# The causal mask of the 384-column score group, moved from four small matmuls to the bias table

## The chip, the core and the metric

One core of one Trainium2 chip runs the whole kernel. The metric is the device time of one execution in microseconds. Three executions of the kernel before took 774.68, 775.28 and 776.92 us; the median is 775.28 us.

## What is computed

Eight batches of eight heads of causal attention (576 positions, head size 64) with a bias that falls with a running sum, then a mixture of eight experts where each token goes to one expert.

```
scores = scale * q @ k.T                       # per head, 576 x 576
cum    = cumsum(max(s, 0))
bias   = -(cum[i] - cum[j])
scores = where(j > i, -1e9, scores + min(bias, 0))
attn   = softmax(scores)                       # rows
o      = attn @ v                              # then heads side by side: 4608 x 512
out[t] = gate[t] * relu(o[t] @ w1[e]) @ w2[e]  # e = argmax of o[t] @ w_gate
```

## The kernel before

Two heads make a pair; there are 32 pairs, worked on one after the other for the first 300 us. After them come the eight experts, which the change doesn't touch. Queries are cut into five groups, named by their number g: rows 128 g to 128 g + 127 for g = 0 to 3, and the last 64 rows of both heads together for g = 4. Group g needs the keys up to its own rows only, so its score widths are 128, 256, 384, 512 and 576 (`TW`, L57).

For each pair and group these steps follow each other:

- S (`scores`, L253, matmuls at L238): TensorE writes the scores of both heads to a PSUM tile named `s`. Each product is made of three terms, high by high, high by low and low by high halves of q and k (`kh`, `kl`). The pool of `s` tiles has two buffers, and the routing of tokens takes buffers of it too (below).
- R (`rowmax`, L278, instruction at L296): VectorE adds the bias table `B` to the scores, scales, and finds the row maximum. There is one instruction per head for g = 0 to 3 (R20 and R21 for group 2) and one for g = 4 (R40), each with a short read of its accumulator behind it.
- X (`expo`, L301): ScalarE takes the exponential. T (`trans`): TensorE turns the result. E (L334 on VectorE, L335 on ScalarE): the turned result is copied to `aT`. AV (`av`, L337): TensorE multiplies with v; XB (`keep`): VectorE copies that product out of PSUM (`xb`).

`B` has one tile per pair with four buffers. For each head it holds six blocks of 128 columns (`UB` = 768): blocks 0 to 3 hold the running sums of the keys, and GpSimd (`causal`, L176) writes masked copies of blocks 0 and 1 to blocks 4 and 5 and masks block 3 in place. Group 0 reads block 4, group 1 blocks 0 and 5, group 3 blocks 0 to 3. Group 2 would need blocks 0 and 1 and a masked block 2, which isn't there: block 2 is needed unmasked by group 3. So TensorE adds the mask of group 2: in `mms` (L227), ahead of the third term, four bf16 matmuls per pair (L233) add the product of `eye` and `tri`, a constant triangle, to the last 128 columns of the scores.

The order of all steps on all engines is written out by hand (`ORDER`, L33): one line of names with a pair offset each, gone through once per pair. On TensorE one pass reads

```
S0:0 [routing] T2:1 T4:1 S2:0 S4:0 T3:0 [routing] T1:0 S3:-1 T0:0 S1:-1 AV:1
```

where `:-1` is the next pair and `:1` the one before. From pair 6 on, each pass holds two routing steps, and each takes an `s` buffer, so the seven users of the two buffers alternate: S2 waits until R00 and R01 have read the buffer of S0, S4 until the first routing step's tile is read, and S3 until R40 has read the buffer of S4. On VectorE the same pass reads XB, R00, R01, a routing copy, E4 (the copy of 640 columns at L334), R20, R21, R40, a routing copy, then R31, R10, R30, R11 of the next pair and E0. The routing steps repeat every four pairs.

`table` (L164) loads `B` from memory by three transfers on SyncE's queue, four pairs ahead; `split` (L200) makes the q and k halves on GpSimd, two pairs ahead. GpSimd's pass is: the select and add of `causal`, `q` (L207), its low half (L212), `qd` (L222), `kl` (L219), and one or two scatters of routed tokens.

Of the kernel before, what the change touches and what calls it, by code (L numbers as in the profile page):

```python
# [8 lines left out]
F32 = mybir.dt.float32  # L9
F32R = mybir.dt.float32r  # L10
BF16 = mybir.dt.bfloat16
# [3 lines left out]
ALU = mybir.AluOpType  # L15
# [4 lines left out]
P, HP = 128, 64  # L20
B, H, S, D = 8, 8, 576, 64
# [33 lines left out]
TURN_AT = {0: 0, 2: 2}  # L55
PIN = True
TW = (128, 256, 384, 512, 576)  # L57
UB, UW = 768, 1536


def disjoint(tc, key, inst):
# [15 lines left out]
class Attention:  # L77
# [18 lines left out]
    def open_pairs(self):  # L96
        nc, rt, ident, low = self.nc, self.rt, self.K["ident"], self.Es[0][:, 0]
        cp, s, raw, cum, zz = self.first
        x = self.ldx.tile([P, 2 * S], F32, name="qk")
        self.st[0] = dict(x=x)  # L100
        for h, e in enumerate((nc.sync, nc.scalar)):
            e.dma_start(x[:, S * h : S * h + S], self.qkv[0][:, S * h : S * h + S])
        for h, e in enumerate((nc.sync, nc.scalar)):
            e.dma_start(raw[64 * h : 64 * h + 64], s)
        self.load(1)
        self.load_v(0)
        self.load(2)
        nc.vector.memset(zz, 0.0)
        nc.scalar.activation(self.sm.tile([P, 1], F32, name="m"), zz[:, :1], AF.Exp)
        nc.gpsimd.memset(low, 0.0)  # L110
        for h in range(2):
            self.keep_causal(low[64 * h : 64 * h + 64], low[64 * h : 64 * h + 64], [[-1, P]])
        self.mixed = cp.tile([P, HP], F32, name="mixed")
        nc.gpsimd.tensor_copy(self.mixed, low[:, :HP])
        b = self.st[0]["B"] = self.tab.tile([P, UW + S], F32, name="B")
        nc.gpsimd.memset(b, 0.0)
        self.causal(0)
        warm = self.ps_s.tile([P, 2, 512], F32, name="s")[:, 0]
        zb = zz.bitcast(BF16)
        for _ in range(WARM):  # L120
            nc.tensor.matmul(warm, zb[:, :P], zb[:, P : P + 512], start=True, stop=True)
        self.cum = cum
        self.sel = cp.tile([P, 3, P], F32, name="sel")
        for x, h, c in (0, 0, slice(0, P)), (1, 65, slice(0, P)), (2, 0, slice(0, HP)), (2, 1, slice(HP, P)):
            nc.vector.tensor_copy(self.sel[:, x, c], ident[:, h : h + 1].broadcast_to([P, c.stop - c.start]))
        self.eye = cp.tile([P, 3, HP], BF16, name="eye")
        nc.vector.memset(self.eye, 0.0)
        nc.vector.tensor_tensor(out=self.eye[:, 1], in0=ident[:, :HP], in1=ident[:, HP:], op=ALU.add)
        self.tri = cp.tile([P, P], BF16, name="tri")
        nc.vector.tensor_copy(self.tri, low)  # L130
        nc.vector.tensor_scalar(out=raw, in0=raw, scalar1=0.0, scalar2=8.0, op0=ALU.max, op1=ALU.mult)
        nc.vector.tensor_tensor_scan(
            out=cum, data0=raw, data1=zz, initial=0.0, op0=ALU.add, op1=ALU.add
        )
        for part in (0, 2, 1, 3, 4):
            self.split(0, part)
        nc.scalar.dma_start(self.K["cum"], cum[:64])
        self.table(1)
        self.load(3)
        self.table(2)  # L140
        self.load_v(1)
        self.table(3)
        self.load_v(2)
        for g in ORD[:2]:
            self.first_bias(g)
        nc.gpsimd.memset(self.Es[MIX][:, S:], 0.0)
        self.LT = rt.tile([P, 640], F32, name="LT", bufs=1)
        nc.gpsimd.memset(self.LT[:, S:], 0.0)
        self.xb, self.sums, self.sumx, self.rr, self.ra = [], [], [], [], []
        for i in range(2):  # L150
            self.xb.append(rt.tile([P, 4, 640], F32, name=f"xb{i}", bufs=1))
            nc.gpsimd.memset(self.xb[i][:, :, S:], 0.0)
            self.sums.append(rt.tile([P, 4, 8], F32, name=f"sums{i}", bufs=1))
            self.sumx.append(rt.tile([P, 4], F32, name=f"sumx{i}", bufs=1))
            self.rr.append(rt.tile([P, 5, 8], F32, name=f"rr{i}", bufs=1))
            nc.gpsimd.memset(self.rr[i][:, 4], 1.0)
            self.ra.append(rt.tile([P, 2, 5, 4], F32, name=f"ra{i}", bufs=1))
# [6 lines left out]
    def table(self, p):  # L164
        nc, cum = self.nc, self.K["cum"]
        t = self.st.setdefault(p, {})["B"] = self.tab.tile([P, UW + S], F32, name="B")
        nc.sync.dma_start(
            t[:, :UW].rearrange("p (h c) -> p h c", h=2)[:, :, :512],
            cum[2 * p : 2 * p + 2, :512].unsqueeze(0).broadcast_to([P, 2, 512]),
        )  # L170
        for h in range(2):
            nc.sync.dma_start(
                t[64 * h : 64 * h + 64, UW:], cum[2 * p + h : 2 * p + h + 1].broadcast_to([64, S])
            )

    def causal(self, p):  # L176
        t = self.st[p]["B"]
        b = t[:, :UW].rearrange("p (h k c) -> p h k c", h=2, c=P)
        self.keep_causal(b[:, :, 4:], b[:, :, :2], [[0, 2], [0, 2], [-1, P]])
        self.keep_causal(b[:, :, 3], b[:, :, 3], [[0, 2], [-1, P]])  # L180
        x = t[:, UW + 512 :]
        self.nc.gpsimd.tensor_tensor(out=x, in0=x, in1=self.mixed, op=ALU.add)

# [40 lines left out]
                    compare_op=ALU.is_ge, fill=0.0, base=base, channel_multiplier=2 * h - 1,  # L224
                )

    def mms(self, groups, diagonal=None, begin=True):  # L227
        for n in range(len(groups[0][1])):
            if n == diagonal:
                for out, eye, tri in ((P, 1, P), (HP, 0, HP)):  # L230
                    for h, (ps, _) in enumerate(groups):
                        r = slice(64 * h, 64 * h + 64)
                        self.nc.tensor.matmul(  # L233
                            ps[:, ps.shape[1] - out :], self.eye[r, eye : eye + 2], self.tri[r, :tri],
                            start=False, stop=False, skip_group_check=True,
                        )
            for out, terms in groups:
                self.nc.tensor.matmul(  # L238
                    out, terms[n][0], terms[n][1], start=begin and n == 0, stop=n == len(terms) - 1, skip_group_check=True
                )  # L240
# [12 lines left out]
    def scores(self, p, g):  # L253
        d = self.st[p]
        w = TW[g]
        if p == 0:
            if ("S", g) not in d:
                self.first_bias(g)
            ps = d["S", g]
        else:  # L260
            ps = d["S", g] = self.ps_s.tile([P, 2, 512], F32, name="s")
        if g == MIX:
            qh, ql = (self.qd[p % 2][:, x].rearrange("p h c -> p (h c)") for x in range(2))
            for a in range(2):
                c = slice(288 * a, 288 * a + 288)
                self.mms([(ps[:, a, :288], [
                    (qh, d["kh"][:, c]), (qh, d["kl"][:, c]), (ql, d["kh"][:, c]),
                ])], begin=p > 0)
            return
        groups = []  # L270
        for h in range(2):
            r = slice(64 * h, 64 * h + 64)
            qh, ql = (d["q"][r, x, P * g : P * g + P] for x in range(2))
            kh, kl = d["kh"][r, :w], d["kl"][r, :w]
            groups.append((ps[:, h, :w], [(qh, kh), (qh, kl), (ql, kh)]))
        self.mms(groups, 2 if g == 2 else None, p > 0)

    def rowmax(self, p, g, h):  # L278
        nc, d, w = self.nc, self.st[p], TW[g]
        ps, t = d["S", g], d["B"]  # L280
        if g == MIX:
            cut = lambda x: x.rearrange("p (a c) -> p a c", a=2)
            units = [(ps[:, :, :288], cut(t[:, UW:]))]
        else:
            cut = lambda x: x
            b = t[:, UB * h : UB * h + UB]
            if g == 1:
                cut = lambda x: x.rearrange("p (k c) -> p k c", c=P)
                b = cut(b)[:, 0:6:5]
            else:  # L290
                b = b[:, 512:640] if g == 0 else b[:, :w]
            units = [(cut(ps[:, h, :w]), b)]
        for x, mask in units:
            z = self.wk.tile([P, S], F32, name="z")
            m = self.sm.tile([P, 1], F32, name="m")
            nc.vector.tensor_tensor_reduce(  # L296
                out=cut(z[:, :w]), in0=x, in1=mask, scale=-0.125, scalar=3.0e38, op0=ALU.add, op1=ALU.min, accum_out=m,
            )
            d["z", g, h] = z, m
# [723 lines left out]
```

## Time and profile before

| what | value |
|---|---|
| median of three executions | 775.28 us |
| the profiled execution, its own time | 778.14 us |
| its span, first to last instruction | 776.4 us |
| mean granted TensorE clock | 0.992 |
| PE busy | 746.7 us (96%) |
| DVE busy | 453.9 us (58%) |
| ACT busy | 418.8 us (54%) |
| POOL busy | 251.7 us (32%) |

PE, DVE, ACT and POOL are TensorE's matmuls, VectorE, ScalarE and GpSimd; SPq is the queue of SyncE, which issues transfers. Busy shares are means over the whole span, attention and experts together. A row of the timeline has the start and the length in us, the engine, the line, the operation, what it writes and reads, its shape, and how many instructions were merged; in brackets stands the idle time of the engine before it and what ended it. Matmuls overlap, and their ends are modelled, so start-to-start distances are the safer measure on PE.

### The profile page before, as it was taken

What the parts mean: (1) busy time and instruction counts of PE and PEld (TensorE: products, weight loads), DVE (VectorE), ACT (ScalarE), POOL (GpSimd) and SP (SyncE); (2) the same over time, 40 slices, a digit from 0 to 9 for tenths busy, and PEclk for the clock granted to TensorE, in tenths of its full rate; (3) what the DMA queues carried; (4) which work ended last, traced back from release to release, by engine and by line L of the source; (5) the groups of instructions that cost most, each with busy time, mean ns of one, the idle gap of its engine ahead of it and who ended that gap; (6) DMA issues with size and microseconds to landing.
All of it is one profiled execution on the core that took longest, in us unless ns stands there. A gap on an engine that the chain in (4) does not pass through costs nothing.

```text
span 776.4 us, 17542 instructions
## 1 busy us (share of the span) xinstructions
PE 746.7 (96%) x6654; PEld 579.6 (75%) x6654; DVE 453.9 (58%) x1232; ACT 418.8 (54%) x1004; POOL 251.7 (32%) x362
## 2 busy tenths in 40 slices
PE   7899999999999997998999999999999999999995
PEld 4667777777777765687887888888888887878874
DVE  6778989888898985752363634422632453634420
ACT  4999999999999986441341523322512432513400
POOL 5665777676767664111001010010011001010011
PEclk9999999999999999999999999999999999999998
DMA  7999677776867543498161634510720442620101
GB/s 245 341 322 294 207 249 225 236 228 211 253 209 237 168 169 125 132 296 285 49 228 71 211 128 161 179 41 18 244 96 28 140 178 69 219 97 22 54 30 41
DMA packets 58015, 130.78 MB, mean 168 GB/s; under 512 B 5487, under 2 KB 6511, under 8 KB 57904
## 3 DMA queue, kind: packets, MB, share of 16 engines
q1 hardware_dynamic: 49216, 105.08, 42.2%
q0 software_dynamic: 5936, 18.92, 6.5%
q10 hardware_dynamic: 2752, 5.33, 2.1%
q8 instruction: 66, 1.08, 0.6%
q14 instruction: 45, 0.37, 0.2%
HBM read 101.30 MB, written 28.27 MB: 167 GB/s over the span
## 4 chain that ended last, share of the span: by engine, by line
issue 40%; PE 38%; DMA 11%; another core or an unknown queue 4%; POOL 3%; POOLq 1%; ACT 1%; DVE 1%; SPq 1%; ACTq 0%; DVEq 0%
PE s L238 12%; PE t L345 10%; PE t L312 7%; DMA out_dram<-y,xr 6%; PE ph L730 3%; PE py L752 3%; POOL out_dram L759 3%; PE s L312 1%; DMA qk<-in_qkv_dram 1%; PE s L388 1%; DMA B<-cum 1%; DMA xr<-xs 1%; DMA aT<-in_s_dram 1%; DMA raw<-in_w_dram 1%
## 5 line engine op out<-in xcount | busy, mean ns | idle before, releaser
L752 PE MATMUL py<-w2t,hT 128*128 128x512 f32 x768 | 181.3, 393 | 1.6 <-PEq L866 1.6
L730 PE MATMUL ph<-xT,w1t 128*128 128x512 f32 x768 | 178.3, 392 | 1.6 <-ACT xT L635 1.2
L308 ACT ACTIVATE E<-z,m 128x512 f32<-128x512 f32 (+4 forms) x288 | 166.8, 583 | 19.7 <-DVE m L296 16.9
L730 PEld LDWEIGHTS ph<-xT,w1t 128*128 128x128 f32 x768 | 143.8, 188 | 33.6 <-issue 2.5
L759 POOL DMA_INDIRECT out_dram<-y,xr x39 | 38.0, 975 | 398.3 <-DVE y L758 333.2
L752 PEld LDWEIGHTS py<-w2t,hT 128*128 128x128 f32 x768 | 142.5, 188 | 31.8 <-issue 2.0
L296 DVE CUSTOM_DVE_ANT_0 z<-s,B 128x512 f32<-128x512 f32 (+3 forms) x224 | 116.5, 543 | 13.2 <-PE s L238 4.7
L345 PE MATMUL t<-aT,v 128*64 128x64 f32 (+4 forms) x1152 | 94.6, 318 | 1.1 <-ACT w1t L657 1.0
L238 PE MATMUL s<-kh,q 64*128 64x128 f32 (+3 forms) x512 | 92.3, 370 | 2.7 <-DVE m L296 2.7
L758 DVE TENSOR_SCALAR y<-py,xr 128x512 f32<-128x512 f32 x35 | 26.3, 751 | 115.1 <-PE py L752 115.1
L732 ACT ACTIVATE hT<-ph 128x512 fp32r<-128x512 f32 x64 | 38.2, 597 | 102.3 <-PE ph L730 102.2
L733 DVE SCALAR_TENSOR_TENSOR hT<-ph,hT 128x512 fp32r<-128x512 f32 x64 | 44.1, 691 | 66.7 <-ACT hT L732 66.7
L312 PE MATMUL t<-ident,E 64*128 64x64 f32 x1600 | 75.4, 227 | 1.9 <-ACT aT L335 0.9
L335 ACT COPY aT<-t 128x1024 f32<-128x1024 f32 (+2 forms) x97 | 73.7, 795 | 6.4 <-PE t L312 6.3
L312 PEld LDWEIGHTS t<-ident,E 64*128 64x128 f32 x1600 | 63.8, 139 | 16.7 <-issue 5.3
L238 PEld LDWEIGHTS s<-kh,q 64*128 64x128 f32 x512 | 52.0, 186 | 29.8 <-DVE aT L334 23.5
L345 PEld LDWEIGHTS t<-aT,v 128*64 128x64 f32 x1152 | 50.5, 137 | 21.4 <-issue 11.1
L308 ACT ACTIVATION_READ_ACCUMULATOR E<-z,m 128x1 f32 x288 | 55.4, 192 | 0.0
L474 POOL DMA_INDIRECT xs<-xr,dsi x40 | 40.0, 999 | 37.1 <-DVE num L974 16.4
L635 ACT ACTIVATE xT<-t 128x512 fp32r<-128x512 f32 x32 | 17.5, 597 | 63.6 <-PE t L702 63.3
L219 POOL TENSOR_TENSOR kl<-qk,kh 128x576 fp32r<-128x576 f32 x30 | 42.6, 1420 | 25.0 <-ACT kh L215 25.0
L334 DVE COPY aT<-t 128x256 f32<-128x256 f32 (+1 forms) x63 | 38.7, 614 | 10.5 <-PE t L312 10.5
(159 smaller groups left out, 965.5 us busy)
## 6 DMA issues: line engine op xcount, KB each, us to landing
raw<-in_w_dram SPq DMA_DIRECT2D x32, 1024.0 KB, 5.6
qk<-in_qkv_dram SPq DMA_DIRECT2D x31, 576.0 KB, 5.3
B<-cum SPq DMA_DIRECT2D x31, 512.0 KB, 4.9
v<-in_qkv_dram SPq DMA_DIRECT2D x32, 320.0 KB, 3.9
B<-cum SPq DMA_DIRECT2D x62, 144.0 KB, 5.1
xr<-xs SPq DMA_DIRECT2D x7, 1028.0 KB, 5.5
xs<-blank ACTq DMA_DIRECT2D x9, 514.0 KB, 8.9
xs<-blank SPq DMA_DIRECT2D x8, 514.0 KB, 8.3
```

The source lines that it names most:

```text
L219: e.tensor_tensor(out=d["kl"], in0=k, in1=d["kh"].bitcast(F32), op=ALU.subtract)
L238: self.nc.tensor.matmul(out, terms[n][0], terms[n][1], start=begin and n == 0, stop=n == len(terms) - 1, skip_group_check=True)
L296: nc.vector.tensor_tensor_reduce(out=cut(z[:, :w]), in0=x, in1=mask, scale=-0.125, scalar=3.0e38, op0=ALU.add, op1=ALU.min, accum_out=m,)
L308: nc.scalar.activation(out, z[:, :w], AF.Exp, bias=m, scale=-1.0, accum_out=total)
L312: self.nc.tensor.transpose(out, src[r], self.K["ident"][r, r])
L335: return self.nc.scalar.copy(o, i)
L345: nc.tensor.matmul(ps[64 * h : 64 * h + 64, bank, lo - 512 * bank : hi - 512 * bank], v[:, kt, h], self.aT[p % 2][:, kt, h, lo:hi], start= ...
L474: ins = self.nc.gpsimd.indirect_dma_start(out=self.K["xs"], out_offset=IndirectOffsetOnAxis(ap=r["dsi"][:n, k : k + 1], axis=0), in_=r["xr ...
L730: nc.tensor.matmul(ps, w[:, a, d, c], x[:, b, d], start=n == 0, stop=n == 11)
L733: nc.vector.scalar_tensor_tensor(out=h[:, 1, f], in0=ps, scalar=0.0, in1=h[:, 0, f].bitcast(F32), op0=ALU.max, op1=ALU.subtract)
L752: self.nc.tensor.matmul(ps, hT[:, a, f, c], w[:, b, f % 4], start=f == 0 and i == 0, stop=f == 7 and i == 2)
L759: disjoint(self.tc, "out", self.nc.gpsimd.indirect_dma_start(out=self.out, out_offset=IndirectOffsetOnAxis(ap=row[:, DM + 1 : DM + 2].bitc ...
```

## The change

The table of each head gets a seventh block (`UB` = 896). The running sums of key blocks 0 and 1 lie in places 0 and 1, those of blocks 2 and 3 in places 3 and 4. GpSimd writes masked block 2 to place 2, masks place 4 in place, and writes masked blocks 0 and 1 to places 5 and 6. Group 2 then reads places 0 to 2 in one piece, and group 3 reads places 0, 1, 3 and 4 as two pieces. The four mask matmuls and their constants are gone. The transfer of both heads' first 512 sums becomes two transfers, one per head, each in pieces of 256 sums. The constant `sel`, used for the first pair alone, moves into a part of `aT` that isn't in use yet.

```diff
-UB, UW = 768, 1536
+UB, UW = 896, 1792
...
-        self.sel = cp.tile([P, 3, P], F32, name="sel")
+        self.sel = self.aT[1].rearrange("p a h c -> p (a h c)")[:, 3 * S : 3 * S + 3 * P].rearrange("p (x c) -> p x c", x=3)
...
-        self.eye = cp.tile([P, 3, HP], BF16, name="eye")
-        nc.vector.memset(self.eye, 0.0)
-        nc.vector.tensor_tensor(out=self.eye[:, 1], in0=ident[:, :HP], in1=ident[:, HP:], op=ALU.add)
-        self.tri = cp.tile([P, P], BF16, name="tri")
-        nc.vector.tensor_copy(self.tri, low)
...
-        nc.sync.dma_start(
-            t[:, :UW].rearrange("p (h c) -> p h c", h=2)[:, :, :512],
-            cum[2 * p : 2 * p + 2, :512].unsqueeze(0).broadcast_to([P, 2, 512]),
-        )
+        for h in range(2):
+            nc.sync.dma_start(
+                t[:, UB * h : UB * h + 768].rearrange("p (a c) -> p a c", a=2)[:, :, :256],
+                cum[2 * p + h, :512].rearrange("(a c) -> a c", a=2).unsqueeze(0).broadcast_to([P, 2, 256]),
+            )
...
-        self.keep_causal(b[:, :, 4:], b[:, :, :2], [[0, 2], [0, 2], [-1, P]])
-        self.keep_causal(b[:, :, 3], b[:, :, 3], [[0, 2], [-1, P]])
+        self.keep_causal(b[:, :, 5:], b[:, :, :2], [[0, 2], [0, 2], [-1, P]])
+        for x, y in (2, 3), (4, 4):
+            self.keep_causal(b[:, :, x], b[:, :, y], [[0, 2], [-1, P]])
...
-            if n == diagonal:
-                for out, eye, tri in ((P, 1, P), (HP, 0, HP)):
-                    for h, (ps, _) in enumerate(groups):
-                        r = slice(64 * h, 64 * h + 64)
-                        self.nc.tensor.matmul(
-                            ps[:, ps.shape[1] - out :], self.eye[r, eye : eye + 2], self.tri[r, :tri],
-                            start=False, stop=False, skip_group_check=True,
-                        )
...
-                b = cut(b)[:, 0:6:5]
+                b = cut(b)[:, 0:7:6]
+            elif g == 3:
+                cut = lambda x: x.rearrange("p (a c) -> p a c", a=2)
+                b = b[:, :768].rearrange("p (a c) -> p a c", a=2)[:, :, :256]
             else:
-                b = b[:, 512:640] if g == 0 else b[:, :w]
+                b = b[:, 640:768] if g == 0 else b[:, :w]
```

On PE, at groups 2 and 4 of one pair in the routing stretch, the order before has the weights and products of the mask between the second and the third term of the 384-column scores (`eye` and `tri` are the constants of the mask):

```order
L312 MATMUL t<-ident,E_109 128x64 x10
L238 MATMUL s<-kh,q 128x384 x2
L238 MATMUL s<-kl,q 128x384 x2
L233 LDWEIGHTS eye
L233 MATMUL s<-tri,eye 128x128
L233 LDWEIGHTS eye
L233 MATMUL s<-tri,eye 128x128
L233 LDWEIGHTS eye
L233 MATMUL s<-tri,eye 128x64
L233 LDWEIGHTS eye
L233 MATMUL s<-tri,eye 128x64
L238 MATMUL s<-kh,q 128x384 x2
```

On PE at the same place, the order of the change:

```order
L304 MATMUL t<-ident,E_109 128x64 x10
L227 MATMUL s<-kh,q 128x384 x2
L227 MATMUL s<-kl,q 128x384 x2
L227 MATMUL s<-kh,q 128x384 x2
L227 MATMUL s<-kh,qd_104 128x288
```

The third term now follows the second directly; nothing else of TensorE's order has moved.

On GpSimd, at the table of pair 1 early in the program, the order before (`mixed` is the mask of group 4, `ramp` a constant of the routing):

```order
L160 AFFINE_SELECT B<-B 128x2x256
L160 AFFINE_SELECT B<-B 128x2x128
L182 TENSOR_TENSOR B<-B,mixed 128x64
L207 CAST q<-qk 128x576
L212 TENSOR_TENSOR q<-qk,q 128x576
L905 IOTA blank 128x1
L912 IOTA ramp 128x8
```

On GpSimd at the same place, the order of the change:

```order
L155 AFFINE_SELECT B<-B 128x2x256
L155 AFFINE_SELECT B<-B 128x2x128 x2
L179 TENSOR_TENSOR B<-B,mixed 128x64
L204 CAST q<-qk 128x576
L209 TENSOR_TENSOR q<-qk,q 128x576
L897 IOTA blank 128x1
L904 IOTA ramp 128x8
```

There is one more select of 2 x 128 columns ahead of everything else that GpSimd does in the pass.

On SyncE's queue, at the first table, the order before and then that of the change (`qk` is the q and k of a pair to come):

```order
L167 DMA B<-cum 128x2x512
L172 DMA B<-cum 64x576 x2
L186 DMA qk<-in_qkv_dram 128x1152
L167 DMA B<-cum 128x2x512
L172 DMA B<-cum 64x576 x2
```

```order
L163 DMA B<-cum 128x2x256 x2
L168 DMA B<-cum 64x576 x2
L183 DMA qk<-in_qkv_dram 128x1152
L163 DMA B<-cum 128x2x256 x2
L168 DMA B<-cum 64x576 x2
```

Each table is issued in four transfers instead of three, and all behind it on that queue stand one issue later.

## Rows read from the trace of the kernel before

**Rows 1.** Busy time by stretch: us, then PE, PEld, DVE, ACT, POOL, clock, DMA

```profile
62.00:302.00 240.00, 237.81 (x3659) 175.11 (x3657) 209.07 (x748) 217.64 (x591) 165.12 (x239) 1.00 0.68 217
```

**Rows 2.** Timeline, PE and DVE, pair 16: S2, mask, S4, R20 to S3

```profile
157.81 0.34 PE L238 MATMUL s<-kl,q 64*128 64x384 f32 x2
...
157.98 0.26 PE L233 MATMUL s<-tri,eye 64*128 64x128 bf16 x4
157.99 0.81 DVE L334 COPY aT<-t 128x640 f32<-128x640 f32 x1
...
158.08 0.42 PE L238 MATMUL s<-kh,q 64*128 64x384 f32 x2
...
158.72 0.55 DVE L296 CUSTOM_DVE_ANT_0 z<-s,B 128x384 f32<-128x384 f32 x1
...
159.19 0.29 PE L238 MATMUL s<-kh,qd 128*128 128x288 f32 x1
159.19 0.08 DVE L296 DVE_READ_ACCUMULATOR2_ANT m<- 128x1 f32 x1
159.19 0.55 DVE L296 CUSTOM_DVE_ANT_0 z<-s,B 128x384 f32<-128x384 f32 x1
...
159.67 0.08 DVE L296 DVE_READ_ACCUMULATOR2_ANT m<- 128x1 f32 x1
159.72 0.76 DVE L296 CUSTOM_DVE_ANT_0 z<-s,B 128x576 f32<-128x576 f32 x1
...
160.40 0.08 DVE L296 DVE_READ_ACCUMULATOR2_ANT m<- 128x1 f32 x1
...
160.63 0.50 PE L238 MATMUL s<-kh,q 64*128 64x512 f32 x2
```

**Rows 3.** Waits on VectorE between 60 and 272 us: sum, times, longest

```profile
DVE xb L334 <- PE t L345: 10.1, 23, 0.7
```

**Rows 4.** Timeline, PE and DVE, pair 18: E4, R20, S4, R40, S3

```profile
176.25 0.82 DVE L334 COPY aT<-t 128x640 f32<-128x640 f32 x1 [1.24 <-PE t L312]
...
177.12 0.56 DVE L296 CUSTOM_DVE_ANT_0 z<-s,B 128x384 f32<-128x384 f32 x1
...
177.66 0.29 PE L238 MATMUL s<-kh,qd 128*128 128x288 f32 x1
...
178.08 0.08 DVE L296 DVE_READ_ACCUMULATOR2_ANT m<- 128x1 f32 x1
178.19 0.76 DVE L296 CUSTOM_DVE_ANT_0 z<-s,B 128x576 f32<-128x576 f32 x1
...
179.10 0.50 PE L238 MATMUL s<-kh,q 64*128 64x512 f32 x2
```

**Rows 5.** Groups by line and shape, to 400 us: busy, mean ns, idle before

```profile
L296 DVE CUSTOM_DVE_ANT_0 z<-s,B 128x512 f32<-128x512 f32 x64 | 44.0, 688 | 7.9 <-ACT aT L335 4.4 <-PE s L238 1.3 <-POOL qd L222 0.9
...
L296 DVE CUSTOM_DVE_ANT_0 z<-s,B 128x384 f32<-128x384 f32 x64 | 33.0, 551 | 4.0 <-PE s L238 3.4 <-ACT E L308 0.2
...
L296 DVE CUSTOM_DVE_ANT_1 z<-s,B 128x256 f32<-128x256 f32 x64 | 26.9, 420 | 3.2 <-ACT E L308 1.5 <-PE s L238 0.6
...
L160 POOL TENSOR_SCALAR_AFFINE_SELECT B<-B 128x256 f32<-128x256 f32 x32 | 13.0, 405 | 0.0
```

**Rows 6.** Timeline, GpSimd, pair 17: the tightest wait ahead of `q`

```profile
167.36 0.66 POOL L207 CAST q<-qk 128x576 fp32r<-128x576 f32 x1 [0.37 <-PE s L238]
```

**Rows 7.** Issues of the table's main transfer: ns min/median/max, first and last start

```profile
L167 SPq DMA_DIRECT2D B<-cum x31: 377/377/438, 11.1 to 259.8; - x31
```

**Rows 8.** Timeline of the start: GpSimd's table of pair 1, `ramp`, S4 of pair 1

```profile
16.54 0.32 POOL L182 TENSOR_TENSOR B<-B,mixed 128x64 f32<-128x64 f32 x1 [0.78 <-DMA B<-cum]
...
19.18 0.17 DVE L926 CAST w<-ramp 128x8 f32<-128x8 int32 x1 [0.25 <-POOL ramp L912]
...
24.07 0.37 PE L238 MATMUL s<-kh,qd 128*128 128x288 f32 x1 [0.42 <-DVE m L296]
```

**Rows 9.** Timeline of the first 5 us: VectorE's cast of `tri` under GpSimd's memset

```profile
2.34 1.85 POOL L116 MEMSET B<- 128x2112 f32 x1
...
2.53 1.74 DVE L130 CAST tri<-E 128x128 bf16<-128x128 f32 x1
```

More of the change, by code (lines that the diff above doesn't have):

```diff
@@ L225, in split, with mms @@
                 )
-    def mms(self, groups, diagonal=None, begin=True):
+    def mms(self, groups, begin=True):
         for n in range(len(groups[0][1])):
-            if n == diagonal:
-                for out, eye, tri in ((P, 1, P), (HP, 0, HP)):
-                    for h, (ps, _) in enumerate(groups):
-                        r = slice(64 * h, 64 * h + 64)
-                        self.nc.tensor.matmul(
-                            ps[:, ps.shape[1] - out :], self.eye[r, eye : eye + 2], self.tri[r, :tri],
-                            start=False, stop=False, skip_group_check=True,
-                        )
             for out, terms in groups:
@@ L275, in scores @@
             groups.append((ps[:, h, :w], [(qh, kh), (qh, kl), (ql, kh)]))
-        self.mms(groups, 2 if g == 2 else None, p > 0)
+        self.mms(groups, p > 0)
     def rowmax(self, p, g, h):
```

## The prediction

> **What bounds the kernel now.** I read the busy time by stretch first, then the timeline of single pairs with PE and DVE side by side, then the waits. Between 62 and 302 us PE is busy for 237.81 of 240 us [rows 1]; read alone, that says that whatever leaves PE shortens the time by its full length. The timeline says something else. In pair 16, S3 starts at 160.63, 0.23 us after R40's accumulator read began at 160.40 [rows 2]; in pair 18 R40 starts at 178.19 and lasts 0.76, and S3 follows at 179.10 [rows 4]. By the trace, S3 stands 0.15 us behind the end of that read in all 25 pairs from 5 to 29, whatever PE did just before: S3 waits until R40 has read S4's buffer. So PE is a part of a loop, not the bound by itself: AV, then the copy of its product (xb) on DVE, R00 to R40 there, then S3, T0, S1 and the next AV on PE.
>
> Who sets R40? Its last input is S4. In pair 16 the last matmul of S4 ends at 159.19 + 0.29 = 159.48 and R40 starts 0.24 later; in pair 18 it ends at 177.95 and R40 starts 0.24 later [rows 2, 4]. The distance is the same in both, while the distance from the read behind R21 isn't: 159.72 - 159.67 = 0.05 and 178.19 - 178.08 = 0.11. An instruction that waits for DVE alone starts with that read (R21 does: 159.19 and 159.19 [rows 2]). So R40 waits for PE, but DVE is nearly as late: it could start R40 only 0.05 us sooner in pair 16, and 0.11 sooner in pair 18. In pair 16 DVE has been busy without a break since xb, which waits for AV's end (23 times between 60 and 272 us [rows 3]). In pair 18, DVE waits 1.24 us for PE ahead of E4, and R20 starts at 177.12, 0.05 after E4's end at 177.07; in pair 16 it starts 0.08 before E4's end (157.99 + 0.81 = 158.80 against 158.72), as instructions in a row do. So in pair 18 R20 and all after it follow PE.
>
> **The change part by part.**
>
> *The mask products.* In pair 16 the second term starts at 157.81, the mask at 157.98, the third term at 158.08 [rows 2]. Without the mask the third term can start where the mask did: 0.10 us per pair, 3.2 us over 32 pairs. Their summed lengths say more, but they overlap. What reaches the end:
> - Pairs 6 to 28 stand in the full loop; the routing steps repeat every four pairs. Six of these 23 (6, 10, to 26) are like pair 18: R20 follows S2, R40 follows S4, DVE has room, so the whole 0.10 counts: 0.6 us.
> - The other 17 are like pair 16: S4 ends 0.10 sooner, but R40 only 0.05 sooner, where DVE's own chain takes over. That is what is late next. In the trace this room is 0.04 to 0.06: 17 x 0.05 = 0.85 us. Bounds: 0, if DVE can't start R40 any sooner, and 1.7.
> - In pairs 2 to 5, R20 follows S2 as in pair 18: 0.4 us. Pairs 29 and 31 too: 0.2. In pair 30 DVE and ACT are late already, and in pairs 0 and 1 the start (below) sets the time: 0.
>
> Together 2.05 us.
>
> *GpSimd's extra select.* One more select of 2 x 128 columns, 0.405 us each [rows 5], in 32 passes. It lies ahead of q, for which GpSimd waits on PE; the shortest of these waits in the loop is 0.37 us [rows 6], and what is left over there (0.04) falls into the wait for kh ahead of kl. What GpSimd makes is used most of a pass later or more. I cost it at nothing in the loop; without that cover it would be 0.4 us per pair.
>
> *One more issue on SyncE's queue, per table.* An issue takes 0.38 to 0.44 us [rows 7]. From pair 4 on, tables are issued three to four passes ahead, and nothing waits for them. At the start it counts: GpSimd waits until 16.54 for the last transfer of pair 1's table, then does q and its low half for pair 2, then `ramp`, for which DVE waits 0.25 us until 19.18; DVE's chain from there ends in S4 of pair 1, which waits for it at 24.07 [rows 8]. One issue later by 0.43 moves all of that by 0.43. Bounds: 0, if the transfers land no later, and 0.8, if the select's 0.4 adds to it. I take 0.43, since at 16.54 the transfer and not the select ends the wait (the extra select fits into the 0.78 before it).
>
> *The two-piece read of group 3.* The nearest row is group 1, whose table is read in two pieces already: 420 ns for 256 columns, against 551 - (688 - 551) = 414 for one piece by the 384 and 512 rows [rows 5]. So 6 ns per instruction, two per pair, ahead of DVE's wait for AV (10.1 us over 23 passes [rows 3], 0.44 each): nothing. Bounds: nothing, and nothing up to 0.2 us per instruction, since 0.4 is covered.
>
> *The rest.* The dropped set-up (eye, tri) ran while DVE waited for the s transfer: nothing. GpSimd's first memset is longer by an eighth of 1.85 us [rows 9], and waits follow it: nothing.
>
> Sum: 2.05 - 0.43 = 1.62 us. The profiled execution took 778.14 us (span 776.4), so 776.5 for it; that execution lies 2.9 above the median of the runs, 775.28, and against the median the forecast is **773.7 us**.
>
> **The rivals.**
>
> *PE pays in full.* R40's room on DVE is larger than the 0.05 that I read, and the start hides the issue: 3.0 us, 772.3; with the start's 0.43, 772.7. For it: PE's busy share, and that R40 keeps the same distance to S4 throughout. Against it: 17 pairs with DVE busy from xb to R40. Chance 0.20.
>
> *DVE takes nearly all.* The 0.05 isn't there: R40 has several semaphores to wait for, and they may cost it that time in any case. Then only the pairs like 18, 2 to 5, 29 and 31 pay: 1.2 - 0.43 = 0.8 us, 774.5. Chance 0.20.
>
> *GpSimd holds VectorE up: slower.* The cast of tri, 128 columns, took 1.74 us and ended at 4.27, just after GpSimd's memset at 4.19 [rows 9]: here one engine stood still for the other. If the extra select does that to DVE inside the chain from xb to R40, each of some 30 pairs loses up to 0.405 us, 12 us in all, less the 1.6: about 785.7. It decides where the select falls: between S3 and xb, DVE's 0.44 of waiting swallows it; after xb nothing does. It falls after the first select, when DVE does xb and R00. Against it: DVE's row maxima of 512 columns take 688 ns on average over 64 [rows 5] although GpSimd works through many of them. Chance 0.03.
> The Trainium skill, page "SBUF — State Buffer", section "Who interferes with whom", says that VectorE and GpSimd share one port pair as an exclusive lock, but that a VectorE instruction with at most one SBUF input, outside the two-port modes, doesn't take it. By that the cast of tri would have been locked out, which rows 9 bear out, and xb and the row maxima, which read PSUM, wouldn't be, so that the rule itself speaks for nothing lost in the loop.
>
> **How the numbers follow.** Forecast 0.57, the rivals 0.20, 0.20 and 0.03. A measurement of this kernel tells about 0.3%, 2.3 us, from no change, so faster means below 772.95. The first rival lies there at 772.3 to 772.7, and the forecast's lower edge (DVE's room nearer to 0.10, the start hidden) reaches it: 0.18 + 0.04 = 0.22. Slower needs the third rival, and 0.01 for a start that costs far more: 0.04. Same: 0.74. The range reaches from the first rival, less 0.4 for the scatter of a median, to the second with the start at 0.8 and a scatter of 0.6 (the three runs shown lie between 0.6 below and 1.6 above their median): 771.9 to 775.7.
>
> **What would show it.** In pair 16's place, the third term starts 0.17 us after the second; R40 starts at the read behind R21 or within 0.02 of it, and not 0.05 later; S3 keeps its 0.15 behind R40's read. In pair 18's place R40 keeps 0.24 to S4 and R20 moves to 0.05 before E4's end. GpSimd's wait ahead of q shrinks by 0.4, and is gone where it was 0.37. S4 of pair 1 starts at about 24.5. The forecast is wrong if R40 still has room everywhere (then it is the first rival), if the row maxima or xb get longer under the select (the third), or if the stretch from 62 to 302 us shrinks by less than 0.7 us or more than 2.

## The result, and the profile after

The changed kernel is slower by 0.6%, where no change to a gain of 0.2% was forecast.

| | median us (runs) | lowest to highest | ratio, 95% interval |
|---|---|---|---|
| before | 775.26 (20) | 773.42 to 779.03 | |
| changed | 781.37 (20) | 775.27 to 786.46 | 1.0062 [1.0042, 1.0082] |

The profiled execution of the changed kernel took 775.63 us (span 773.9), one of its fastest; a second profile of both kernels follows among the experiments. Where the time went is read from the start of S2 of single pairs in the timelines, and from the first ReLU copy of the experts:

| us | S2 of pair 1 | pair 2 | pair 4 | pair 5 | pair 28 | first expert | span |
|---|---|---|---|---|---|---|---|
| before | 22.66 | 31.77 | 49.66 | 58.27 | 265.53 | 320.5 | 776.4 |
| changed | 24.49 | 33.77 | 55.88 | 64.43 | 269.54 | 320.8 | 773.9 |
| difference | +1.83 | +2.00 | +6.22 | +6.16 | +4.01 | +0.3 | -2.5 |

So the loop from pair 5 to pair 28 did gain, 2.15 us, and more than 6 us were lost before it. Of what this execution wins after pair 28, the 3.7 us up to the first expert come again in the second profile below (3.3 us there); the rest, in the experts, doesn't. The forecast had no such gain. The runs issues and maskback below, which have the mask products on TensorE, reach the first expert 1.7 and 1.9 us sooner after pair 28 than the kernel before, so at least that much isn't the mask's. Where the gain comes from is open.

The loop first. The stretch of [rows 1] in the changed kernel, same columns:

```profile
62.00:302.00 240.00, 237.39 (x3591) 176.54 (x3589) 209.19 (x754) 220.00 (x602) 176.56 (x269) 1.00 0.72 223
```

TensorE is as full as before. Pair 16, the place of [rows 2], PE and DVE in the timeline (start, length, engine, line, operation):

```profile
162.78 0.34 PE L227 MATMUL s<-kl,q 64*128 64x384 f32 x2
162.96 0.34 PE L227 MATMUL s<-kh,q 64*128 64x384 f32 x2
...
163.23 0.40 PE L227 MATMUL s<-kh,qd 128*128 128x288 f32 x1
...
164.00 0.29 PE L227 MATMUL s<-kh,qd 128*128 128x288 f32 x1
...
164.65 0.08 DVE L288 DVE_READ_ACCUMULATOR2_ANT m<- 128x1 f32 x1
164.65 0.75 DVE L288 CUSTOM_DVE_ANT_0 z<-s,B 128x576 f32<-128x576 f32 x1
...
165.33 0.08 DVE L288 DVE_READ_ACCUMULATOR2_ANT m<- 128x1 f32 x1
...
165.56 0.50 PE L227 MATMUL s<-kh,q 64*128 64x512 f32 x2
```

R40 now starts with the read behind R21 (164.65 and 164.65; 0.05 later before), S4's last product has ended 0.36 before it instead of 0.24, and S3 keeps its 0.15 behind R40's read: DVE sets R40 here, as forecast.

The loss. Busy time from 17 to 62 us, before and then changed:

```profile
17.00:25.00 8.00, 5.81 (x87) 4.41 (x85) 7.15 (x28) 7.03 (x19) 6.79 (x14) 1.00 1.04 318
25.00:30.00 5.00, 4.87 (x77) 3.35 (x76) 3.76 (x15) 5.00 (x14) 2.87 (x5) 1.00 1.07 307
30.00:40.00 10.00, 9.24 (x130) 6.27 (x126) 6.52 (x23) 8.60 (x25) 5.99 (x10) 1.00 1.06 366
40.00:50.00 10.00, 9.73 (x152) 7.08 (x150) 7.44 (x28) 9.42 (x28) 5.90 (x11) 1.00 1.03 312
50.00:62.00 12.00, 11.80 (x174) 8.66 (x172) 10.66 (x35) 11.07 (x31) 7.83 (x12) 1.00 1.04 334
```

```profile
17.00:25.00 8.00, 4.34 (x69) 3.69 (x67) 5.68 (x25) 6.15 (x16) 6.34 (x14) 0.87 1.07 267
25.00:30.00 5.00, 4.89 (x64) 3.68 (x63) 3.63 (x12) 4.36 (x12) 2.63 (x4) 0.86 1.08 247
30.00:40.00 10.00, 7.49 (x100) 4.96 (x98) 5.79 (x20) 6.83 (x20) 5.37 (x9) 1.00 1.07 319
40.00:50.00 10.00, 8.15 (x116) 5.79 (x116) 5.74 (x22) 6.82 (x22) 6.00 (x12) 1.00 1.04 325
50.00:62.00 12.00, 11.12 (x162) 7.74 (x160) 9.27 (x34) 11.67 (x31) 6.53 (x10) 1.00 0.99 307
```

The columns are those of [rows 1]. The DMA engines are full in both. Between 30 and 50 us TensorE is busy for 15.64 us where it was 18.97, and ScalarE for 13.65 where it was 18.02. Who waits for what is in ScalarE's timeline of pairs 2 and 3, before and then changed:

```profile
29.80 0.62 ACTq L195 DMA_DIRECT2D xs<-blank  x1
...
31.70 0.58 ACTq L195 DMA_DIRECT2D xs<-blank  x1
32.33 0.72 ACT L308 ACTIVATE E<-z,m 128x512 f32<-128x512 f32 x1 [1.41 <-DMA qk<-in_qkv_dram]
...
39.03 0.55 ACTq L195 DMA_DIRECT2D xs<-blank  x1
...
39.62 0.63 ACTq L195 DMA_DIRECT2D xs<-blank  x1
```

```profile
33.63 2.42 ACTq L192 DMA_DIRECT2D xs<-blank  x2
36.10 0.72 ACT L300 ACTIVATE E<-z,m 128x512 f32<-128x512 f32 x1 [3.17 <-DMA wg<-in_wg_dram]
...
43.93 3.19 ACTq L192 DMA_DIRECT2D xs<-blank  x2
47.16 0.72 ACT L300 ACTIVATE E<-z,m 128x512 f32<-128x512 f32 x1 [3.18 <-DMA xs<-blank]
...
48.00 0.56 DVE L288 CUSTOM_DVE_ANT_0 z<-s,B 128x384 f32<-128x384 f32 x1 [1.64 <-ACT E L300]
48.02 0.71 PE L304 MATMUL t<-ident,E 64*128 64x64 f32 x16 [1.42 <-ACT E L300]
```

The transfers `xs<-blank` are nine fills of 514 KB that write blank rows for the experts, two per pair from pair 2 on (`fill`, L192; L195 before). ScalarE issues them, between two of its exponentials. In the changed kernel it waits over 3 us at that place in pairs 2 and 3, then R21 on DVE (48.00) and T3 on TensorE (48.02) wait for ScalarE. The releaser is a transfer, and the chain that ended last says which (start, length, what):

```profile
13.66 6.84 DMA B<-cum
...
20.51 7.81 DMA B<-cum
...
28.34 7.12 DMA wg<-in_wg_dram
...
35.48 11.06 DMA xs<-blank
...
46.57 0.54 ACTq L192
...
47.16 1.20 ACT E L300 x4
```

Each transfer there is issued when an earlier one has landed. That is the program: it gives the transfers of SyncE and ScalarE eight completion counters in turn, and the instruction that issues a transfer first waits until the one eight places before it has landed. With the numbers of the transfers in program order:

```
kernel before, 5 transfers of SyncE + 2 fills per pair
  31 fill   waits for 23 table      33 fill   waits for 25 qk
  38 fill   waits for 30 table      40 fill   waits for 32 v
changed kernel, 6 transfers of SyncE + 2 fills per pair
  36 fill   waits for 28 v          38 fill   waits for 30 wg
  44 fill   waits for 36 fill       46 fill   waits for 38 fill
```

Before, seven transfers make a pair, and a fill stands behind a table or `v` transfer (144 or 320 KB); only the second fill stands behind `qk` (576 KB), which is the wait of 1.41 us above. With one transfer more there are eight, as many as counters, and from pair 3 on each fill waits for the fill of the pair before, which took 11.06 us to land (35.48 to 46.54) while a pair takes 8.6. In pairs 4 to 6 the fills are issued in 0.54 to 0.63 us each, without such a wait: ScalarE stalls twice, and not once per pair.

The start, the place of [rows 8]:

```profile
17.84 0.32 POOL L179 TENSOR_TENSOR B<-B,mixed 128x64 f32<-128x64 f32 x1 [1.12 <-DMA B<-cum]
...
20.46 0.17 DVE L918 CAST w<-ramp 128x8 f32<-128x8 int32 x1 [2.05 <-POOL ramp L904]
...
25.79 0.61 PE L227 MATMUL s<-kh,qd 128*128 128x288 f32 x1
```

It is the chain that was named, but the transfer lands 1.30 us later (17.84 against 16.54), not 0.43, and S4 of pair 1 comes at 25.79 instead of 24.07, with TensorE at a granted clock of 0.87 between 17 and 25 us and 0.86 from there to 30, where it had 1.00. SyncE's issues of the table's last two transfers, before and then changed:

```profile
11.56 1.12 SPq L172 DMA_DIRECT2D B<-cum  x2
```

```profile
11.86 1.13 SPq L168 DMA_DIRECT2D B<-cum  x2
```

They start 0.30 later; the other 1.0 us lies between there and GpSimd's add (5.98 us against 4.98).

### The profile page after: what moved, and what is told of

It is laid out like the page before. It is cut to its first block, busy times and chain, and to the rows that moved or that the text cites. A ratio compares the mean times of both kernels' runs of the same rounds, so it can differ in the third digit from the quotient of the medians.

```text
span 773.9 us, 17411 instructions
## 1 busy us (share of the span) xinstructions
PE 740.8 (96%) x6526; PEld 577.8 (75%) x6526; DVE 449.8 (58%) x1229; ACT 418.6 (54%) x1004; POOL 263.2 (34%) x394
## 4 chain that ended last, share of the span: by engine, by line
issue 39%; PE 36%; DMA 12%; POOL 4%; another core or an unknown queue 4%; DVE 1%; POOLq 1%; ACT 1%; SPq 0%; ACTq 0%; DVEq 0%
PE s L227 11%; PE t L337 10%; DMA out_dram<-y,xr 6%; PE t L304 6%; PE ph L722 3%; PE py L744 3%; POOL out_dram L751 3%; DMA B<-cum 2%; DMA xs<-blank 1%; PE s L304 1%; POOL q L209 1%; PE s L380 1%; DMA wg<-in_wg_dram 1%; DMA xr<-xs 1%
## 5 line engine op out<-in xcount | busy, mean ns | idle before, releaser
L227 PE MATMUL s<-kh,q 64*128 64x128 f32 (+3 forms) x512 | 90.2, 362 | 5.3 <-DVE m L288 4.7
L288 DVE CUSTOM_DVE_ANT_0 z<-s,B 128x128 f32<-128x128 f32 (+2 forms) x160 | 71.5, 484 | 7.7 <-ACT E L300 4.4
L288 DVE CUSTOM_DVE_ANT_1 z<-s,B 128x512 f32<-128x512 f32 (+1 forms) x128 | 64.8, 553 | 12.1 <-DMA qk<-in_qkv_dram 3.0
```

The source lines that it names most:

```text
L227: self.nc.tensor.matmul(out, terms[n][0], terms[n][1], start=begin and n == 0, stop=n == len(terms) - 1, skip_group_check=True)
L288: nc.vector.tensor_tensor_reduce(out=cut(z[:, :w]), in0=x, in1=mask, scale=-0.125, scalar=3.0e38, op0=ALU.add, op1=ALU.min, accum_out=m,)
```

## The experiments

**First: what costs, the transfers, GpSimd, or TensorE's clock?** Theory D blames the table's transfers, G GpSimd's added select, C TensorE's clock. Four kernels beside the one before (777.96 us in these runs).

*nomask*: the kernel before without the mask products.

```
-        self.mms(groups, 2 if g == 2 else None, p > 0)
+        self.mms(groups, None, p > 0)
```

> The kernel before with only the four mask products of the 384-column group left out (the part of the computation that it drops is the mask of that group's diagonal block), the table, its transfers and GpSimd as before. Theory D (the gain of TensorE is there in full, and the table's transfers, doubled in number and in pieces of half the size, take it back in the first 62 us while the DMA engines have no room): ratio to before about 0.996, 771.5 to 773 us, and the stretch from 20 to 62 us as before. Rival C (TensorE, with less to do, loses clock at the start or between attention and experts): 777 us or more, and a granted clock below that of before. Rival G (GpSimd's added select): 0.996 as in D, so this run doesn't tell D from G.

Measured: 794.62 us, 1.0199 [1.0155, 1.0243]. As a total this run says nothing: without that mask the attention's result is another one, tokens can go to other experts, and from the first expert to the end it takes 471 us (317.1 to 788.1) instead of 456 (320.5 to 776.4). Its attention part can be used: S2 of pair 28 stands 204.91 us behind S2 of pair 5, against 207.26 before. The clock was not lower (0.992 in both profiles).

*maskback*: the changed kernel with the mask products and their two constants put back.

```
...
-        self.mms(groups, p > 0)
+        self.mms(groups, 2 if g == 2 else None, p > 0)
```

> The changed kernel with the four mask products put back on TensorE (the block is then masked twice): table, transfers and GpSimd of the changed kernel, TensorE's work of before. Theory D and rival G: about 784 us, ratio to before 1.010 to 1.013, since what costs is all there and the 3 us of gain are gone. Rival C: about 775 us, as before, since TensorE has its work again.

Measured: 783.13 us, 1.0057 [1.0027, 1.0088]. Against C, which wanted 775. It is less than the 1.010 to 1.013 that D and G wanted; the 2.2 us of the loop are gone (S2 of pair 28 stands 207.31 behind pair 5), but the total doesn't show it within its interval.

*issues*: the kernel before, with the table's transfer for two heads issued as two, 2 KB pieces kept.

```
-        nc.sync.dma_start(
-            t[:, :UW].rearrange("p (h c) -> p h c", h=2)[:, :, :512],
-            cum[2 * p : 2 * p + 2, :512].unsqueeze(0).broadcast_to([P, 2, 512]),
-        )
+        for h in range(2):
+            nc.sync.dma_start(
+                t[:, UB * h : UB * h + 512], cum[2 * p + h : 2 * p + h + 1, :512].broadcast_to([P, 512])
+            )
```

> The kernel before with its table's transfer for both heads issued as two, one per head, rows of 2 KB kept: one issue more per table, packets of the same size. Theory D if the number of issues on SyncE costs: 779 to 783 us (ratio 1.005 to 1.010), with the stall in pairs 2 and 3. Theory D if the small pieces cost: within 0.2% of before. Rivals C and G: as before, 775 us.

Measured: 784.26 us, 1.0064 [1.0035, 1.0093]: the whole loss, from one transfer more, with the same bytes, the same pieces, GpSimd and TensorE as before. Its chain that ended last is that of the changed kernel:

```profile
14.51 7.10 DMA B<-cum
...
21.63 7.54 DMA B<-cum
29.18 6.94 DMA wg<-in_wg_dram
...
36.14 11.40 DMA xs<-blank
...
47.56 0.54 ACTq L195
```

In this profile S2 of pair 5 stands 7.7 us behind that of the kernel before; 4.5 of them are there by pair 2 (36.25 against 31.77), before ScalarE's first wait at a fill ends (36.75), and 3.2 come between pair 2 and pair 5. So the start belongs to the loss, and not only the fills.

And since maskback, with twice as many pieces of half the size, loses no more (1.0057), the size of the pieces costs nothing that the totals can tell.

*contig*: the changed kernel with each head's 512 sums in one piece (blocks 0 to 3), loaded by one transfer as before; GpSimd copies blocks 2 and 3 (3 masked) to 5 and 6, masks 2 in place, and writes masked 0 and 1 to 3 and 4. Group 3 reads blocks 0, 1, 5 and 6.

```
...
-        self.keep_causal(b[:, :, 5:], b[:, :, :2], [[0, 2], [0, 2], [-1, P]])
-        for x, y in (2, 3), (4, 4):
-            self.keep_causal(b[:, :, x], b[:, :, y], [[0, 2], [-1, P]])
+        self.keep_causal(b[:, :, 5:], b[:, :, 2:4], [[0, 2], [-P, 2], [-1, P]], P)
+        self.keep_causal(b[:, :, 2], b[:, :, 2], [[0, 2], [-1, P]])
+        self.keep_causal(b[:, :, 3:5], b[:, :, :2], [[0, 2], [0, 2], [-1, P]])
...
```

> The changed kernel with another layout: each head's 512 sums lie in one piece, loaded by one transfer with 2 KB rows as before; GpSimd writes the masked block 2 in its place after it has copied blocks 2 and 3 (3 masked) behind, three selects, one of them of four blocks, so that GpSimd does 0.28 us per pair more than in the changed kernel. Theory D: the whole gain without the cost, ratio to before 0.995 to 0.997 (771.5 to 773 us). Rival G: 782 us or more, slower than the changed kernel, since GpSimd has more to do. Rival C: about 781 us.

Measured: 775.88 us, 0.9972 [0.9941, 1.0004]. G falls: GpSimd does more than in the changed kernel, and the loss is gone. S2 of pair 28 stands 205.31 us behind pair 5. ScalarE issues its fills in 0.54 to 0.63 us each in this profile, without a wait of over 1 us behind any.

**Second: is it ScalarE's wait for a counter?** Theory L says so; P blames the 1 KB pieces. The kernel before took 777.44 us in these runs.

*fill_sp*: the changed kernel with the fills issued by SyncE.

```
-        self.nc.scalar.dma_start(
+        self.nc.sync.dma_start(
             self.K["xs"][lo : lo + TAIL].rearrange("(p k) c -> p k c", k=2),
```

> The changed kernel with the same nine fills, at the same places of the program, issued by SyncE instead of ScalarE; counters and pieces as in the changed kernel. Theory L: the wait of some 3 us moves from ScalarE to SyncE, where only later loads stand behind it; ScalarE's two waits of over 3 us are gone, ratio to before 0.998 to 1.002. If it is the DMA engines' rate that costs and not ScalarE's wait: 1.006 as the changed kernel.

Measured: 777.38 us, 1.0003 [0.9984, 1.0021], below the changed kernel's interval. The same stretches as above, and SyncE's fills:

```profile
30.00:40.00 10.00, 9.81 (x140) 6.76 (x138) 7.31 (x28) 9.60 (x26) 5.56 (x9) 1.00 1.06 281
40.00:50.00 10.00, 9.81 (x138) 6.60 (x134) 7.29 (x25) 9.59 (x29) 8.46 (x16) 1.00 1.07 266
```

```profile
35.54 2.23 SPq L192 DMA_DIRECT2D xs<-blank  x2
...
47.37 1.50 SPq L192 DMA_DIRECT2D xs<-blank  x2
```

The profiled execution is the fastest of the twelve (773.67 us). In it TensorE is full from 30 us on, at less traffic than in either kernel (281 and 266 GB/s): the rate of the DMA engines was not what TensorE lacked. The wait stands on SyncE now. The Trainium skill, page "DMA: Bandwidth & Descriptors", section "Anatomy of one DMA — SWDGE (gpsimd) path", says that any wait on a semaphore happens on the issuing sequencer and not in the DMA engines; the waits of ScalarE (3.18 us) and their end when SyncE issues agree, though that section is on GpSimd's queue and these are ScalarE's and SyncE's.

The start is as late here as in the changed kernel (S2 of pair 1 at 24.29, of pair 2 at 33.61), so a late start alone doesn't make the loss. But the median is no better than before, although the loop is as short as in the changed kernel (S2 of pair 28 stands 205.1 us behind pair 5): about the loop's 2 us are still lost in a typical execution, and this profile of the fastest one doesn't show where.

*fill_late*: the changed kernel with the fills three at a time from pair 4 on.

```
-            if name == "X11" and 2 <= p and self.nfill <= E:
-                for _ in range(2):
+            if name == "X11" and 4 <= p and self.nfill <= E:
+                for _ in range(3):
```

> The changed kernel with the nine fills issued three at a time from pair 4 on instead of two from pair 2 on, still by ScalarE. Theory L: no wait of ScalarE for a fill in pairs 2 and 3, S2 of pair 4 at 52 to 53 us instead of 55.88, while the 1.8 us that the start lost by S2 of pair 1 stay: ratio to before 0.998 to 1.002. If the late start is the cause of the whole loss and the fills are not: 1.006 as the changed kernel. Theory P: 1.004 or more.

Measured: 781.59 us, 1.0053 [1.0028, 1.0079]. The total was forecast wrongly. Pairs 2 and 3 did as expected (S2 of pair 4 at 51.14), but the wait moved along with the fills: ScalarE stands idle for 3.93 us ahead of an exponential at 63.45, with two fills issued at the end of it (the profile names no releaser), and for 3.19 at 74.52, waiting for `B<-cum`, and pair 6 comes 15.5 us after pair 5. I had looked for the fills' place among full DMA engines, and not at which transfer stands eight places before each: for three fills in a pair, again transfers issued within the last pair.

*mixone*: the changed kernel with the two transfers of the mixed sums joined, to come back to five per pair.

```
-        for h in range(2):
-            nc.sync.dma_start(
-                t[64 * h : 64 * h + 64, UW:], cum[2 * p + h : 2 * p + h + 1].broadcast_to([64, S])
-            )
+        nc.sync.dma_start(
+            t[:, UW:], cum[2 * p : 2 * p + 2].unsqueeze(1).broadcast_to([2, 64, S])
+        )
```

> The changed kernel with the two transfers of the table's mixed sums joined into one, so that SyncE issues five transfers per pair as before; the 1 KB pieces, the mask by GpSimd and all else stay. Theory L (the program gives its transfers eight completion counters in turn, so a transfer waits until the eighth before it has landed; with six transfers of SyncE and two fills per pair a fill stands just eight behind the fill of the pair before, and ScalarE, which issues it, waits for that to land): the fills stand behind the same kinds of transfer as before, the stalls of 3 us in pairs 2 and 3 go, ratio to before 0.995 to 0.998. Theory P (pieces of 1 KB cost the DMA engines their rate): 1.003 or more, near the changed kernel's 1.006.

*contig_mixone*: contig with the same joined transfer.

> The layout with one 512-sum piece per head (run contig) and the mixed sums in one transfer: four transfers of SyncE per pair, one fewer than before. Theory L: each counter comes round later, issues wait less, the start comes no later than before: ratio to before 0.993 to 0.996, faster than contig. If the number of transfers plays no part: as contig, 0.997.

Measured, in this order: 850.98 us, 1.0945 [1.0909, 1.0982], and 847.47 us, 1.0900 [1.0871, 1.0929]. All theories missed, since the joined transfer is itself slow, and so these two runs say nothing on the number of transfers. In the chain of mixone (first fence) transfers take up to 20.75 us, and while they are under way the DMA engines' mean share falls to 0.13 (second fence, columns as above):

```profile
62.53 15.93 DMA v<-in_qkv_dram
...
82.86 20.75 DMA B<-cum
```

```profile
74.00:78.00 4.00, 2.21 (x26) 1.64 (x22) 1.75 (x8) 0.00 (x0) 2.81 (x6) 1.00 0.13 51
```

A share of 0.13 of 16 engines is the time of 2.1 engines, and of the 93 packets that start in that stretch 56 have 2,304 bytes, the length of a row of the joined transfer. So the work of about two engines is under way there, and most of it is that transfer's. The profile doesn't name the engines of a transfer, so that they are always the same two, with all others queued behind, is argued and not shown. The Trainium skill, page "DMA: Bandwidth & Descriptors", section "Why a DMA increments its semaphore by 16 and not by 1", gives a rule that fits: a transfer is spread over the largest number of engines up to 16 that divides the slowest dimension of both sides, which here is 2 on the source's side. An estimate by that rule: two engines would carry half of the 288 KB each and 1/16 of a pair's other 1,408 KB, 232 KB; at the 334 GB/s of 16 engines in the stretch from 50 to 62 us before, 20.9 each, that is 11.4 us per pair. Measured are 10.7 (S2 of pair 5 at 88.39, of pair 28 at 334.25).

**Third: does moving the fills help any kernel, and do both parts add up?** The kernel before took 776.72 us in these runs.

*before_fill_sp*: the kernel before with the edit of fill_sp.

> The kernel before with its nine fills issued by SyncE instead of ScalarE, nothing else: what the move is worth where five transfers and two fills stand in a pair. Theory L: the fills of the kernel before found their counters free (0.54 to 0.63 us each, one wait of 1.41 us), so there is little to win: ratio 0.997 to 1.000, S2 of pair 5 at 57 to 58.5 us against 58.27. If moving the fills helps any kernel by 4 us, whatever its transfers per pair: 0.995.

Measured: 779.76 us, 1.0037 [1.0010, 1.0064], slower, where no change or a small gain was expected. So issuing the fills by SyncE is no gain in itself: it won only where they had held up ScalarE. In its profile TensorE runs at 0.63 between 25 and 30 us, before any fill, and S2 of pair 5 comes at 59.45; whether the 0.4% is that or the loads behind SyncE's waits isn't settled.

*contig_fill_sp*: the layout of contig and the fills by SyncE.

> The layout of contig (one 512-sum piece per head, one transfer for both heads, three selects) with the fills issued by SyncE. Theory L: the loop gains its 2 us as in the changed kernel (S2 of pair 28 stands 205.1 to 205.4 us behind S2 of pair 5), no wait of ScalarE for a fill, ratio to before 0.994 to 0.997: faster than both kernels. If the start or the clock there takes it back: 0.998 or more.

Measured: 773.53 us, 0.9951 [0.9926, 0.9976], the only version that is clearly faster than both kernels. S2 of pair 28 stands 205.23 us behind pair 5.

**Last: where does a typical execution lose?** Both kernels once more, unedited, on one chip.

*after_again*

> The changed kernel once more, unedited, for a second profile: its first one took 775.63 us, while its median is 781.37. Theory L: the length of ScalarE's wait for a fill is that of the fill's landing and differs from run to run; where the execution is near the median, S2 of pair 5 stands later than 64.43 us, by up to the missing 5 us, and ScalarE's waits for fills are longer or more than two; S2 of pair 28 stands again 205.1 us behind it. If the loss is in the change to the experts instead: S2 of pair 5 near 64.4 us, and from S2 of pair 31 to the end more than 474.5 us, with a lower clock there.

*before_again*

> The kernel before once more, unedited, beside it on the same chip: S2 of pair 5 within 1.5 us of 58.27, S2 of pair 28 207.2 to 207.3 us behind it, no wait of ScalarE for a fill of over 1.5 us. What differs from the first profile is what one profile can tell by chance.

Measured: 788.69 us (span 787.0) and 782.95 (781.2). The difference is 5.8 us of span, as between the medians, and in the timelines: S2 of pair 5 at 69.00 against 58.54 (+10.5), from there to pair 28 206.29 against 210.17 (-3.9), from there to the first expert 53.7 against 57.0 (-3.3), and the first expert 64.5 against 62.1 (+2.4). The loss stands ahead of pair 5 as L said, and is larger than in the first profile; 3.0 us of it are there by pair 2 (35.35 against 32.36). At the first expert 3.2 us are left, and the 2.4 in an expert that the change doesn't touch have no cause shown. ScalarE's wait and the clock behind it in after_again:

```profile
45.75 3.37 ACTq L192 DMA_DIRECT2D xs<-blank  x2
49.17 0.72 ACT L300 ACTIVATE E<-z,m 128x512 f32<-128x512 f32 x1 [4.77 <-DMA xs<-blank]
```

```profile
40.00:50.00 10.00, 6.61 (x86) 4.56 (x86) 4.89 (x17) 5.23 (x16) 7.24 (x13) 1.00 1.05 276
50.00:62.00 12.00, 11.11 (x115) 7.30 (x116) 6.13 (x21) 9.45 (x27) 3.59 (x6) 0.72 0.99 287
```

The fill took 12.65 us to land this time, and after TensorE had been idle for 3.4 of 10 us its granted clock fell to 0.72 in the next stretch: pair 4 came 15.35 us after pair 3, not 8.6. The loops of 205.1 and 207.3 us that I had expected did not repeat: in both second profiles every fourth pair was longer from about pair 9 and pair 13 on, by 0.55 us before and by 0.28 changed. Why is open; the -3.9 between pairs 5 and 28 is larger by it than the first profile's -2.15.

## Why the prediction was wrong

**The step that failed** is "One more issue on SyncE's queue, per table": "From pair 4 on, tables are issued three to four passes ahead, and nothing waits for them." Nothing waits for these tables' data, but something waits for their place. The transfers share eight counters, and a transfer more per pair made ScalarE's fills wait: in pair 2 for `v` and `wg`, in pair 3 for the fills of pair 2 (3.17 and 3.18 us in the first profile, 3.10 and 4.77 in the second). The term was costed at 0.4 us of SyncE's own time; issues, which adds that transfer alone, measures 1.0064 (5.0 us by 777.96), and fill_sp, which takes ScalarE out of the wait, gives back what the change had lost (1.0003), though not the loop's gain. The profile before had the sign of it: ScalarE's 1.41 us for `qk` after a fill. I read the waits of the engines that the change touches, not those of the other queue that shares its counters.

**The start** was the right chain, mis-sized: 0.43 forecast, at most 0.8; 1.30 at GpSimd and 1.72 at S4 of pair 1 measured. The forecast priced SyncE's issue, which comes 0.30 later, and took the time to landing as unchanged; that grew by 1.0 us (5.98 and 6.05 from the issue to GpSimd's add in the changed kernel's two profiles, 4.98 and 4.84 before). In issues, with 2 KB pieces, it is 5.01, in fill_late, with 1 KB pieces, 5.18, so whether the pieces do it is open. A start can be as late without that transfer: in contig GpSimd's add begins at 16.48, and S2 of pair 1 still comes at 23.96 and that of pair 5 at 61.28, 3.0 us behind the kernel before. There TensorE is at the lower of its two levels (1.2 GHz, 0.50) ahead of pair 1:

```profile
15.00:17.00 2.00, 2.00 (x7) 1.38 (x5) 1.04 (x4) 1.29 (x6) 1.93 (x5) 0.50 0.97 360
```

The first profile of the changed kernel has 1.00 in that stretch. So how much of the start's loss is the transfer's in a typical execution is open.

**The mask products** were mis-sized. From the second term to S4's first product pair 16 takes 0.45 us (162.78 to 163.23) and pair 18 takes 0.44; before it was 0.62 in both. Pair 16's second term began at 157.81 [rows 2], and its S4 here:

```profile
158.43 0.40 PE L238 MATMUL s<-kh,qd 128*128 128x288 f32 x1
```

So a mask costs 0.17 to 0.18 of TensorE's time, not the 0.10 between two starts, and the third term behind it is longer too (0.42 before [rows 2], 0.34 now). In pairs like 18 the whole of it reached the end: the period of that pair fell from 8.74 to 8.56. In the pairs like 16 it was 0.06 to 0.07 (9.71 to 9.64, 8.77 to 8.71, 8.78 to 8.71), close to the 0.05 to which DVE's chain was to hold it. Together 2.15 us over 23 pairs, where 1.45 was forecast. maskback, with the products put back, has the 207.3 us of before, and nomask, which only leaves them out, 204.9, so this gain is theirs.

**Right at nothing** were the two-piece read (686 ns for 512 columns, 688 before [rows 5]) and the added select in the loop: of GpSimd's waits ahead of `q`, the shortest one is gone, and contig, whose selects take 1.71 us per pair instead of 1.36, has a loop of 205.31 us against 205.11.

**The rivals.** The first one, TensorE pays in full, has the loop's size nearly right for the wrong reason: DVE does cap most pairs. The second, DVE takes nearly all, is out. The third had the right sign with the wrong engine: no row maximum got longer, and contig, with more work on GpSimd, is the faster kernel. None of them was the queue, and a chance of 0.04 for slower was too small for a change that adds a transfer per pair while the DMA engines are full. The range's upper end comes to 775.5 by its own terms (775.28 - 1.2 + 0.8 + 0.6) and not to 775.7; 781.37 is outside either.

## What to carry to other kernels

Where a program gives its transfers a fixed set of counters in turn, count the transfers of one period of the loop against the counters before adding one: what stands exactly that many places before a transfer decides how long its issuer waits, and an engine that computes should not be that issuer. The DMA engines' busy share shows none of this (1.03 to 1.07 between 30 and 50 us in both kernels); the chain that ended last does, as transfers that start when another lands. A few instructions taken from a full engine are priced from the start of what stands ahead of them to the start of what comes next but one, since what follows them may be lengthened too.

## What was not expected of the hardware

- A stall's price was not its own length alone. Where TensorE had been idle for 3.4 of 10 us, its granted clock fell to 0.72 in the 12 us behind (after_again); in the first profile it had been idle for 2.5 and 1.85 of 10 and kept 1.00. The idle time alone doesn't tell the two apart: issues had 2.5 of 10 idle between 40 and 50 us and 0.87 in the 12 us behind. Two executions of one kernel stood 6.2 and 10.5 us behind the kernel before at pair 5.
- A transfer of 288 KB from two rows, in place of two of 144 KB from one row each, cost 70 us over 31 tables (mixone, 850.98 against 781.37).
- With the four bf16 products of the mask ahead of them, the float32 products of the third term took 0.42 us in the timeline, without them 0.34.
